# How a cached-attention and SwiGLU decode kernel loads w_down, the fourth group of wo, and its last tiles

## The chip, the cores and the metric

The kernel runs on one core of one Trainium2 chip. A core has TensorE (PE, matrix products into PSUM), VectorE (DVE), ScalarE (ACT), GpSimd (POOL) and SyncE (SP), which here does nothing but issue DMAs, and sixteen DMA engines that move data from HBM into SBUF. The metric is the device time of one execution in microseconds; the median of three runs counts.

## What is computed

One token is decoded. A is multi-head attention over a long cache, B a SwiGLU feed-forward block, and the output is a gated mix of both:

```python
g = sigmoid((x * gate_w).sum(-1))
q = (x @ wq).reshape(H, Dh)                   # 32 heads of 128, D = 512
scores = einsum("hd,hkd->hk", q, k_cache) * Dh**-0.5
o = einsum("hk,hkd->hd", softmax(scores), v_cache)   # 65536 positions a head
a = o.reshape(H * Dh) @ wo                    # wo: 4096 x 512
b = (silu(x @ w_gate) * (x @ w_up)) @ w_down  # w_down: 1792 x 512
out = g * a + (1 - g) * b
```

All inputs are bf16. The K and V caches are 512 MiB each, and each of their bytes is used once; all weights together are some 14 MB.

## The kernel before

**Tiles.** The caches are cut into tiles of 128 partitions x 16384 elements (4 MB, 32 KB a partition); a head has four K tiles and four V tiles, and there are 128 of each. All tiles live in one ring of five buffers (`big`), which also holds wq, w_gate with w_up (`gu_t`), w_down (`wd_t`) and, at the end, the second half of wo (`wo_t`). A tile can be loaded when the tile five before it in the ring has been used up.

**Work on a tile.** For a K tile, VectorE multiplies by the query and halves the products three times (`products`, lines 240 and 244), and TensorE sums the rest with 16 matmuls against an identity (`scores`, line 254). After the fourth K tile of a head come maximum, exponentials and row sums (`row_max`, `exponentials`, `total`, `weight`). For a V tile, TensorE accumulates 32 matmuls (`values`, line 302) into `O_ps`, four positions and 512 columns at a time. After the fourth V tile of a head, `head_copy` (line 315, and 317 for the last head) brings `O_ps` to SBUF, `head_column` (lines 323 and 330) turns it into a scaled column `oT` by four small products, and `project` (line 335) multiplies it by this head's rows of wo and adds it to `a_ps`. The heads 0 to 15 are projected as they come, with wo in four groups of four heads (`wo_tiles`); the heads 16 to 31 are projected after the last V tile, with `wo_end`.

**Order.** The program is written in the order in which each engine is to work (`manual_schedule`); nothing is reordered. The list `steps` says which K tile and which V tile belong to a step; V runs one head behind K, and by step 40 and later some more. A step issues its K tile, then wo's group if it is due, then its V tile, all on SP's queue, and then the work. Step 2 issues w_down behind K tile 2, and places `feed_forward_mid` (line 209: the products with w_down); step 3 issues wo's first group; the fourth group is issued at V tile 40, between a K and a V tile.

**Completion signals.** The DMAs of the kernel take eight completion semaphores in turn (numbers 100, 102, 104 and 106 to 110 in the trace). A DMA that takes a semaphore waits, on SP, until the DMA that had it before, eight issues earlier, has landed in full. A DMA over 128 partitions raises its semaphore sixteen times in the trace, one over 8 partitions eight times.

**Where before and after differ.** `wd_sb` (lines 136 to 146) lies on 64 partitions, 28 rows of w_down on each, and is loaded by eight DMAs of 8 partitions (every fourth partition). The activations `hT` come on 128 partitions, 14 columns; two matmuls against every second column of the identity turn them into 64 partitions and 28 columns (`h_ps`, line 202), and 28 matmuls on 64 partitions follow. The last V tile is loaded in five pieces, the one before it in two; `wo_end` is loaded in five.

Of the kernel before, what the change touches and what calls it, by code (L numbers as in the profile page):

```python
# [8 lines left out]
ACT = mybir.ActivationFunctionType  # L9
ALU = mybir.AluOpType  # L10
AXIS = mybir.AxisListType
P = 128
# [3 lines left out]
NB = 128  # L16
# [9 lines left out]
def kernel(  # L26
# [14 lines left out]
    nc = tc.nc  # L41
    bf16 = mybir.dt.bfloat16
    f32 = mybir.dt.float32

    _, H, Sk, Dh = A_k_cache.shape
    D = A_x.shape[2]
    F = B_w_gate.shape[1]
    KT = D // P
    FT = F // P
    G = Sk // (NB * P)  # L50
    NBH = Sk // P
    N = H * G
# [4 lines left out]
    consts = ctx.enter_context(tc.tile_pool(name="consts", bufs=1))  # L57
# [7 lines left out]
    psum_m = ctx.enter_context(tc.tile_pool(name="psum_m", bufs=2, space=bass.MemoryType.PSUM))  # L65
# [3 lines left out]
    def big(name):  # L69
        return ring.tile([P, NB * Dh], bf16, name=name, tag="big")  # L70
# [12 lines left out]
    ident_b = consts.tile([P, P], bf16, name="ident_b")  # L83
# [14 lines left out]
    a_ps = psum_a.tile([1, D], f32, name="a_ps")  # L98

    K_tiles, V_tiles, S_tiles, P_tiles, O_tiles = {}, {}, {}, {}, {}  # L100

    def load(dst, cache, n, name, cuts=(0, NB)):
        h, g = divmod(n, G)
        t = big(name)
        view = t.rearrange("p (j d) -> p j d", d=Dh)
        src = cache[0, h, g * NB * P : (g + 1) * NB * P, :].rearrange("(p j) d -> p j d", j=NB)
        for a, b in zip(cuts[:-1], cuts[1:]):
            nc.sync.dma_start(out=view[:, a:b, :], in_=src[:, a:b, :])
        dst[n] = view
# [24 lines left out]
    nc.sync.dma_start(out=wgu_sb[:, 0], in_=B_w_gate.rearrange("(p t) f -> p t f", t=KT))  # L134
    nc.sync.dma_start(out=wgu_sb[:, 1], in_=B_w_up.rearrange("(p t) f -> p t f", t=KT))
    wd_t = big("wd_t")
    HP = P // 2
    GT = F // HP
    wd_sb = wd_t[:HP, : GT * D].rearrange("p (t n) -> p t n", t=GT)
    wd_rows = B_w_down.rearrange("(p t) n -> p t n", t=GT)  # L140

    def load_wd(*which):
        for i in which:
            lo = (0, 1, 2, 3, 32, 33, 34, 35)[i]
            part = slice(lo, lo + 29, 4)
            nc.sync.dma_start(out=wd_sb[part], in_=wd_rows[part])

    with nc.allow_non_contiguous_dma(reason="small"):
        nc.sync.dma_start(out=gwT, in_=gate_w.rearrange("(p t) -> p t", t=KT))
    load_wd(0, 1)  # L150
    WG = 4
    wo_tiles = {}

    WH = H // 2
    wo_end = []

    def load_wo_end(cuts):
        t = big("wo_t")[:, : (H - WH) * D].rearrange("p (h n) -> p h n", n=D)
        rows = A_wo[WH * P :, :].rearrange("(h p) n -> p h n", p=P)
        for a, b in zip(cuts[:-1], cuts[1:]):  # L160
            nc.sync.dma_start(out=t[:, a:b, :], in_=rows[:, a:b, :])
        wo_end.append(t)

    def load_wo(g):
        wo_tiles[g] = wo_pool.tile([P, WG, D], bf16, name="wo_sb")
        rows = A_wo[g * WG * P : (g + 1) * WG * P, :]
        nc.sync.dma_start(out=wo_tiles[g], in_=rows.rearrange("(h p) n -> p h n", p=P))

    def feed_forward_in():

# [18 lines left out]
    def feed_forward_mid(gu_sb, eg):  # L189
        nc.vector.tensor_scalar_add(eg, eg, 1.0)  # L190
        nc.vector.reciprocal(eg, eg)
        hprod = consts.tile([P, FT], f32, name="hprod")
        nc.vector.tensor_tensor(out=hprod, in0=gu_sb[:, :FT], in1=eg, op=ALU.mult)
        hT = consts.tile([P, FT], bf16, name="hT")
        nc.vector.tensor_tensor(out=hT, in0=hprod, in1=gu_sb[:, FT:], op=ALU.mult)
        xg = consts.tile([P, KT], f32, name="xg")
        nc.vector.tensor_tensor(out=xg, in0=xT, in1=gwT, op=ALU.mult)
        xs = consts.tile([P, 1], f32, name="xs")
        nc.vector.tensor_reduce(out=xs, in_=xg, axis=AXIS.X, op=ALU.add)
        h_ps = psum_m.tile([HP, GT], f32, name="h_ps", tag="misc")  # L200
        for r in range(2):
            nc.tensor.matmul(
                h_ps[:, r * FT : (r + 1) * FT], lhsT=ident_b[:, r::2], rhs=hT, start=True, stop=True
            )
        h2 = consts.tile([HP, GT], bf16, name="h2")
        nc.scalar.activation(out=h2, in_=h_ps, func=ACT.Copy)
        b_ps = psum_m.tile([1, D], f32, name="b_ps", tag="misc")
        for t in range(GT):
            nc.tensor.matmul(  # L209
                b_ps, lhsT=h2[:, t : t + 1], rhs=wd_sb[:, t, :], start=(t == 0), stop=(t == GT - 1)  # L210
            )
        g_ps = psum_m.tile([P, 1], f32, name="g_ps", tag="misc")
        nc.tensor.matmul(g_ps, lhsT=ones_f, rhs=xs, start=True, stop=True)
        eg2 = consts.tile([P, 1], f32, name="eg2")
        nc.scalar.activation(out=eg2, in_=g_ps, func=ACT.Exp, scale=-1.0)
        return b_ps, eg2
# [13 lines left out]
    def products(n, a=0, b=NB):  # L230

        h = n // G
        K = K_tiles[n][:, a:b, :]
        qb = q_bc[:, h * Dh : (h + 1) * Dh]
        q_rep = bass.AP(
            tensor=qb.tensor,
            offset=qb.offset,
            ap=[list(qb.ap[0]), [0, b - a], [1, Dh]],
        )
        yield nc.vector.tensor_tensor(out=K, in0=K, in1=q_rep, op=ALU.mult)  # L240
        half = Dh
        while half > WIDTH:
            half //= 2
            yield nc.vector.tensor_tensor(  # L244
                out=K[:, :, 0:half], in0=K[:, :, 0:half], in1=K[:, :, half : 2 * half],
                op=ALU.add,
            )
# [43 lines left out]
    def weight(h, tot_ps):  # L291
        recip = small.tile([P, 1], f32, name="recip")
        nc.vector.reciprocal(recip, tot_ps)  # L293
        nc.vector.tensor_tensor(out=rg[:, h : h + 1], in0=recip, in1=gval, op=ALU.mult)
# [39 lines left out]
    def project(h):  # L334
        nc.tensor.matmul(  # L335
            a_ps,
            lhsT=oT[:, h : h + 1],
            rhs=wo_tiles[h // WG][:, h % WG, :] if h < WH else wo_end[0][:, h - WH, :],
            start=False,
            stop=(h == H - 1),  # L340
        )
# [3 lines left out]
    v = 0  # L345
# [9 lines left out]
    for n, v in steps:  # L355
        if n is not None and n > 1:
            load(K_tiles, A_k_cache, n, "K_t")
        if n == 2:
            load_wd(2, 3, 4, 5, 6, 7)
        if n == 3:  # L360
            load_wo(0)
        if v is not None:
            if v % (WG * G) == 2 * G and v // (WG * G) + 1 < WH // WG:
                load_wo(v // (WG * G) + 1)
            load(V_tiles, A_v_cache, v, "V_t", (0, NB) if v < N - 2 else (0, 64, NB) if v < N - 1 else (0, 32, 64, 96, 112, NB))
            if v == N - 1:
                load_wo_end((0, 4, 8, 12, 14, 16))
        if n == 2:
            ff = feed_forward_mid(*ff)
        halves = (0, NB // 2)  # L370
        vector = iter(()) if n is None else products(n)
        if n == 0:
            vector = (i for a in halves for i in products(n, a, a + NB // 2))
        top_of = None
        if n is None:
            top_of = H - 1 if S_tiles else None
        elif n % G == 0 and n > 0:
            top_of = n // G - 1
            vector = (i for a in halves for i in products(n, a, a + NB // 2))
        if top_of is not None:  # L380
            next(vector, None)
            mT_ps = row_max(top_of)
            next(vector, None)
            exponentials(top_of, mT_ps)
        for _ in vector:
            pass
        if n == 1:
            ff = feed_forward_in()
        if n == 3:
            feed_forward_out(*ff)  # L390
        if tot_ps is not None:
            weight(*tot_ps)
            tot_ps = None
        if done is not None:
            head_column(done, head_copy(done))
        if v is not None:
            values(v)
        if top_of is not None:
            tot_ps = top_of, total(top_of)
        if n is not None:  # L400
            scores(n)
        if done is not None and done < WH:
            project(done)
        done = v // G if v is not None and v % G == G - 1 else None
    O_last = head_copy(H - 1, last=True)
    for h in range(WH, WH + 4):
        project(h)
    head_column(H - 1, O_last)
    for h in range(WH + 4, H):
        project(h)  # L410

    out_sb = consts.tile([1, D], bf16, name="out_sb")
    nc.vector.tensor_copy(out=out_sb, in_=a_ps)
    nc.sync.dma_start(out=out[0], in_=out_sb)


# [28 lines left out]
```

## Time and profile before

| what | value |
|---|---|
| median of 3 runs | 2534.58 us (2534.54 to 2534.76) |
| the profiled execution | 2534.51 us, of it 2532.6 us from the first to the last instruction |
| VectorE busy | 2175.5 us (86% of the span) |
| TensorE busy | 1742.4 us (69%), mean granted clock 0.749 |
| ScalarE busy | 75.9 us (3%) |
| DMA | 1088.63 MB in 42884 packets, mean 430 GB/s |

A profile page gives, for each engine, the busy time, and then the span in forty slices with a digit for the busy tenths of each. Its chain of work goes back from the last instruction, at each step to what released it. The other answers used are the chain in order of time (start, length, what), the timeline (start, length, engine, line, operation, and in brackets the idle time before it and what ended it), and windows, which give for each stretch the busy time and number of instructions of PE, PEld (weight loads), DVE, ACT and POOL, then TensorE's granted clock, the DMA engines' busy share and GB/s. "SPq" is SP's queue. L302 is line 302 of the kernel. The trace also records each DMA packet with its size, start and duration, and each rise of a completion semaphore.

The DMA issues of the kernel, with the size of one:

| tile | DMAs | KB each |
|---|---|---|
| K_t | 127, and 2 halves | 4096, 2048 |
| V_t | 126, 2 halves, 3 and 2 smaller | 4096, 2048, 1024, 512 |
| wo_sb | 4 | 512 |
| wd_t | 8 | 224 |
| wo_t | 3 and 2 | 512, 256 |

### The profile page before, as it was taken

Reading aid. Unit: us, or ns where it says so; the run is one execution under the profiler, and the core shown is the slowest. Engines: PE = TensorE matmul, PEld = TensorE weight load, DVE = VectorE, ACT = ScalarE, POOL = GpSimd, SP = SyncE. Lnnn points to the kernel's source line nnn. Section 1 sums busy time; section 2 is a strip of 40 time slices with the busy share of each in tenths; the row PEclk is TensorE's granted clock in tenths of the full one; section 3 lists DMA queues with packets and bytes.
Section 4 is the critical chain, followed back from the end, with each engine's and each line's share of the span. In section 5 each row is a group of like instructions: output and inputs, shape, how many; then the busy total and the mean of one; then the engine's idle time right before and its main releaser. Section 6 shows DMA issues by size and latency. Waiting matters only on the chain.

```text
span 2532.6 us, 15260 instructions
## 1 busy us (share of the span) xinstructions
PE 1742.4 (69%) x6738; PEld 712.1 (28%) x6738; DVE 2175.5 (86%) x784; ACT 75.9 (3%) x207; POOL 0.7 (0%) x6
## 2 busy tenths in 40 slices
PE   4677666776677666676776677667666776677679
PEld 2222222222222222222222223222222232222223
DVE  7998888888888999998888888888888888888860
ACT  1000000000000000000000000000000000000000
POOL 0000000000000000000000000000000000000000
PEclk7677777777777676677777777777777777777779
DMA  9999999999999999999999999999999999999998
GB/s 415 433 433 430 433 433 433 432 430 435 432 432 434 431 433 432 432 433 433 432 434 433 432 434 433 432 432 434 432 431 434 433 430 434 434 431 433 434 432 339
DMA packets 42884, 1088.63 MB, mean 430 GB/s; under 512 B 4737, under 2 KB 8834, under 8 KB 9090
## 3 DMA queue, kind: packets, MB, share of 16 engines
q1 hardware_dynamic: 42674, 1087.66, 99.7%
q8 instruction: 53, 0.87, 0.1%
q14 instruction: 13, 0.11, 0.0%
q10 hardware_dynamic: 144, 0.00, 0.0%
HBM read 1087.64 MB, written 0.00 MB: 429 GB/s over the span
## 4 chain that ended last, share of the span: by engine, by line
DMA 68%; PE 22%; DVE 10%; issue 1%; ACT 0%; DVEq 0%; SPq 0%
DMA V_t<-in_A_v_cache_dram 61%; PE O_ps L302 20%; DMA K_t<-in_A_k_cache_dram 5%; DVE K_t L240 5%; DVE K_t L244 5%; PE S_ps L254 1%; DMA wo_t<-in_A_wo_dram 1%; DMA wq_t<-in_A_wq_dram 0%; PE qg_ps L117 0%; DVE m L266 0%; PE oh_ps L323 0%; PE a_ps L335 0%; PE a_ps L227 0%; ACT P_sb L279 0%; DVE top L275 0%
## 5 line engine op out<-in xcount | busy, mean ns | idle before, releaser
L302 PE MATMUL O_ps<-V_t,P_sb 128*4 128x512 bf16 x4096 | 1157.3, 453 | 496.8 <-DMA V_t<-in_A_v_cache_dram 494.3
L240 DVE TENSOR_TENSOR K_t<-K_t,q_bc 128x16384 bf16<-128x16384 bf16 (+1 forms) x160 | 1117.2, 6983 | 254.4 <-DMA K_t<-in_A_k_cache_dram 232.9
L244 DVE TENSOR_TENSOR K_t<-K_t 128x4096 bf16<-128x4096 bf16 (+3 forms) x480 | 1030.9, 2148 | 14.3
L302 PEld LDWEIGHTS <-P_sb 128*4 128x4 bf16 x4096 | 393.9, 97 | 1241.0 <-issue 897.5
L254 PE MATMUL S_ps<-K_t,ident_b 128*128 128x128 bf16 x2048 | 466.0, 394 | 107.0 <-DVE K_t L244 106.9
L254 PEld LDWEIGHTS <-ident_b 128*128 128x128 bf16 x2048 | 227.6, 115 | 330.0 <-issue 140.2
L323 PE MATMUL oh_ps<-ident_f,O_sb 4*128 4x1 f32 x256 | 57.9, 343 | 74.1 <-ACT O_sb L315 74.1
L323 PEld LDWEIGHTS oh_ps<-ident_f,O_sb 4*128 4x128 f32 x256 | 55.2, 314 | 83.7 <-ACT O_sb L315 78.9
L270 PE MATMUL mT_ps<-diag,ones_f 128*128 128x128 f32 x64 | 23.6, 468 | 79.8 <-ACT diag L268 79.8
L268 ACT ACTIVATE diag<-ident_f,m 128x128 f32<-128x128 f32 x32 | 12.8, 401 | 2099.3 <-DVE m L266 2099.3
L317 DVE COPY O_sb<-O_ps 4x256 f32<-4x256 f32 x1 | 0.4, 414 | 52.1 <-ACT O_sb L315 52.1
L270 PEld LDWEIGHTS mT_ps<-diag,ones_f 128*128 128x128 f32 x64 | 14.7, 285 | 95.6 <-ACT diag L268 95.6
L266 DVE TENSOR_REDUCE m<-S_ps 128x1 f32<-128x512 f32 x32 | 21.9, 683 | 7.4 <-PE S_ps L254 7.4
L315 ACT ACTIVATE O_sb<-O_ps 4x512 f32<-4x512 f32 (+1 forms) x32 | 18.1, 566 | 131.0 <-PE O_ps L302 131.0
L279 ACT ACTIVATE P_sb<-S_ps,bias 128x512 bf16<-128x512 f32 x32 | 22.0, 687 | 1.0
L117 PE MATMUL qg_ps<-wq_t,X_bc 128*128 128x512 bf16 x32 | 8.6, 436 | 13.2 <-DMA wq_t<-in_A_wq_dram 13.2
L293 DVE RECIPROCAL recip<-tot_ps 128x1 f32<-128x1 f32 x32 | 5.1, 160 | 12.2 <-PE tot_ps L288 12.2
L209 PE MATMUL b_ps<-wd_t,h 64*1 64x512 bf16 x28 | 12.1, 629 | 4.3 <-DMA K_t<-in_A_k_cache_dram 4.3
L288 PEld LDWEIGHTS tot_ps<-rowsum,ones_f 128*128 128x128 f32 x64 | 9.5, 188 | 14.0 <-issue 14.0
L288 PE MATMUL tot_ps<-rowsum,ones_f 128*128 128x1 f32 x64 | 12.2, 260 | 0.0
L330 ACT ACTIVATE oT<-oh_ps,rg 128x1 bf16<-128x1 f32 x32 | 8.4, 263 | 76.6 <-PE oh_ps L323 76.6
L227 PE MATMUL a_ps<-b_sb,ones_f 1*1 1x512 f32 x2 | 1.9, 1032 | 12.1 <-ACT b_sb L226 12.1
(42 smaller groups left out, 73.8 us busy)
## 6 DMA issues: line engine op xcount, KB each, us to landing
K_t<-in_A_k_cache_dram SPq DMA_DIRECT2D x127, 4096.0 KB, 35.3
V_t<-in_A_v_cache_dram SPq DMA_DIRECT2D x126, 4096.0 KB, 29.1
wq_t<-in_A_wq_dram SPq DMA_DIRECT2D x1, 4096.0 KB
K_t<-in_A_k_cache_dram SPq DMA_DIRECT2D x2, 2048.0 KB, 16.8
V_t<-in_A_v_cache_dram SPq DMA_DIRECT2D x2, 2048.0 KB
V_t<-in_A_v_cache_dram SPq DMA_DIRECT2D x3, 1024.0 KB, 29.4
wo_sb<-in_A_wo_dram SPq DMA_DIRECT2D x4, 512.0 KB, 17.3
gu_t<-in_B_w_gate_dram SPq DMA_DIRECT2D x1, 1792.0 KB
```

The source lines that it names most:

```text
L209: nc.tensor.matmul(b_ps, lhsT=h2[:, t : t + 1], rhs=wd_sb[:, t, :], start=(t == 0), stop=(t == GT - 1))
L240: yield nc.vector.tensor_tensor(out=K, in0=K, in1=q_rep, op=ALU.mult)
L244: yield nc.vector.tensor_tensor(out=K[:, :, 0:half], in0=K[:, :, 0:half], in1=K[:, :, half : 2 * half], op=ALU.add,)
L254: nc.tensor.matmul(S_tiles[h][:, g * NB : (g + 1) * NB], lhsT=ident_b, rhs=K_tiles[n][:, :, c], start=(c == 0), stop=(c == WIDTH - 1),)
L266: nc.vector.tensor_reduce(out=m, in_=S_tiles[h], axis=AXIS.X, op=ALU.max)
L268: nc.scalar.activation(out=diag, in_=ident_f, func=ACT.Copy, scale=m)
L270: nc.tensor.matmul(mT_ps, lhsT=ones_f, rhs=diag, start=True, stop=True)
L279: nc.scalar.activation(out=P_tiles[h], in_=S_tiles[h], func=ACT.Exp, bias=bias, scale=scale, accum_out=rowsum[:, h : h + 1],)
L288: nc.tensor.matmul(tot_ps, lhsT=ones_f, rhs=rowsum[:, h : h + 1], start=True, stop=True)
L302: nc.tensor.matmul(O_tiles[h], lhsT=P_tiles[h][:, g * NB + j : g * NB + j + 4], rhs=V_tiles[n][:, j : j + 4, :], start=(g == 0 and j == 0) ...
L315: nc.scalar.activation(out=O_sb[:, :cut], in_=O_ps[:, :cut], func=ACT.Copy)
L323: nc.tensor.matmul(oh_ps, lhsT=O_sb[:, c * Dh : (c + 1) * Dh], rhs=ident_f[0:4, c : c + 1], start=(c == 0), stop=(c == 3),)
```

## The change

w_down moves to 128 partitions with 14 rows each and is loaded by one DMA behind K tile 2, the third K tile; the turn of `hT` goes, and 14 matmuls on 128 partitions take the place of 28 on 64. wo's fourth group (`g == 3`) is loaded by six DMAs of 112, 8, 4, 2, 1 and 1 partitions. The last V tile comes in three pieces (64, 48 and 16 of its 128 columns of 128 elements) and wo's second half in three (7, 6 and 3 heads). After the last V tile, the last head's column is made first, and then all sixteen products with wo; the output is copied half by VectorE, half by ScalarE.

```diff
     wd_t = big("wd_t")
-    HP = P // 2
-    GT = F // HP
-    wd_sb = wd_t[:HP, : GT * D].rearrange("p (t n) -> p t n", t=GT)
-    wd_rows = B_w_down.rearrange("(p t) n -> p t n", t=GT)
-
-    def load_wd(*which):
-        for i in which:
-            lo = (0, 1, 2, 3, 32, 33, 34, 35)[i]
-            part = slice(lo, lo + 29, 4)
-            nc.sync.dma_start(out=wd_sb[part], in_=wd_rows[part])
+    wd_sb = wd_t[:, : FT * D].rearrange("p (t n) -> p t n", t=FT)
...
-    load_wd(0, 1)
...
     def load_wo(g):
         wo_tiles[g] = wo_pool.tile([P, WG, D], bf16, name="wo_sb")
         rows = A_wo[g * WG * P : (g + 1) * WG * P, :]
-        nc.sync.dma_start(out=wo_tiles[g], in_=rows.rearrange("(h p) n -> p h n", p=P))
+        rows = rows.rearrange("(h p) n -> p h n", p=P)
+        cuts = (0, P) if g < WH // WG - 1 else (0, 112, 120, 124, 126, 127, 128)
+        for a, b in zip(cuts[:-1], cuts[1:]):
+            nc.sync.dma_start(out=wo_tiles[g][a:b], in_=rows[a:b])
...
-        h_ps = psum_m.tile([HP, GT], f32, name="h_ps", tag="misc")
-        for r in range(2):
+        b_ps = psum_m.tile([1, D], f32, name="b_ps", tag="misc")
+        for ft in range(FT):
             nc.tensor.matmul(
-                h_ps[:, r * FT : (r + 1) * FT], lhsT=ident_b[:, r::2], rhs=hT, start=True, stop=True
-            )
-        h2 = consts.tile([HP, GT], bf16, name="h2")
-        nc.scalar.activation(out=h2, in_=h_ps, func=ACT.Copy)
-        b_ps = psum_m.tile([1, D], f32, name="b_ps", tag="misc")
-        for t in range(GT):
-            nc.tensor.matmul(
-                b_ps, lhsT=h2[:, t : t + 1], rhs=wd_sb[:, t, :], start=(t == 0), stop=(t == GT - 1)
+                b_ps,
+                lhsT=hT[:, ft : ft + 1],
+                rhs=wd_sb[:, ft, :],
+                start=(ft == 0),
+                stop=(ft == FT - 1),
             )
...
         if n == 2:
-            load_wd(2, 3, 4, 5, 6, 7)
+            nc.sync.dma_start(out=wd_sb, in_=B_w_down.rearrange("(p t) n -> p t n", t=FT))
...
-            load(V_tiles, A_v_cache, v, "V_t", (0, NB) if v < N - 2 else (0, 64, NB) if v < N - 1 else (0, 32, 64, 96, 112, NB))
+            load(V_tiles, A_v_cache, v, "V_t", (0, NB) if v < N - 2 else (0, 64, NB) if v < N - 1 else (0, 64, 112, NB))
             if v == N - 1:
-                load_wo_end((0, 4, 8, 12, 14, 16))
+                load_wo_end((0, 7, 13, 16))
...
     O_last = head_copy(H - 1, last=True)
-    for h in range(WH, WH + 4):
+    head_column(H - 1, O_last)
+    for h in range(WH, H):
         project(h)
-    head_column(H - 1, O_last)
-    for h in range(WH + 4, H):
-        project(h)
 
     out_sb = consts.tile([1, D], bf16, name="out_sb")
-    nc.vector.tensor_copy(out=out_sb, in_=a_ps)
+    nc.vector.tensor_copy(out=out_sb[:, : D // 2], in_=a_ps[:, : D // 2])
+    nc.scalar.activation(out=out_sb[:, D // 2 :], in_=a_ps[:, D // 2 :], func=ACT.Copy)
     nc.sync.dma_start(out=out[0], in_=out_sb)
```

## The prediction

> **What bounds the kernel now.** First the page's busy shares in forty slices, to ask whether the transfers or an engine are full.
>
> ```profile
> DMA  9999999999999999999999999999999999999998
> GB/s 415 433 433 430 433 433 433 432 430 435 432 432 434 431 433 432 432 433 433 432 434 433 432 434 433 432 432 434 432 431 434 433 430 434 434 431 433 434 432 339
> ```
>
> The sixteen DMA engines are full to the last slice. So what counts is the bytes that each must move, and the last one to finish. Next the chain of waits over the last 57 us (start, length, what), which sets the end.
>
> ```profile
> 2472.70 31.39 DMA V_t<-in_A_v_cache_dram
> ...
> 2504.16 20.87 DMA wo_t<-in_A_wo_dram
> 2525.03 0.04 issue
> 2525.07 1.02 PE a_ps L335 x4
> 2526.09 0.98 PE oh_ps L323 x8
> 2527.07 2.69 PE a_ps L335 x12
> 2529.76 0.02 issue
> 2529.79 0.68 DVE out_sb L413
> ```
>
> The gate is V tile 125, issued at 2472.70 and landed at 2504.09; call that landing L. The chain then names wo, but the timeline (start, length, engine) shows TensorE just as late:
>
> ```profile
> 2504.14 20.88 PE L302 MATMUL O_ps<-V_t,P_sb 128*4 128x512 bf16 x96 [1.62 <-DMA V_t<-in_A_v_cache_dram]
> 2525.11 0.37 ACT L315 ACTIVATE O_sb<-O_ps 4x256 f32<-4x256 f32 x1 [29.29 <-PE O_ps L302]
> 2525.52 0.41 DVE L317 COPY O_sb<-O_ps 4x256 f32<-4x256 f32 x1 [52.13 <-ACT O_sb L315]
> ```
>
> From L, TensorE runs tiles 125 to 127 without a break (96 starts 0.216 us apart). So the end is L + 28.5 us, and two questions remain: where L goes, and what the tail behind it becomes.
>
> Why is L late? Each 128-partition load raises sixteen completion signals, one for each DMA engine. The trace's records give those of tile 125:
>
> ```
> 2487.52 2487.56 | 2494.24 2494.27 2494.35 2494.36 2494.56 2494.78 2495.28 2495.92 2495.97 2496.01 2496.59 | 2500.18 2503.01 2504.09
> ```
>
> The mean is 2495.5; the load waits for one engine that is 8.5 us behind it. Two sources of the spread can be followed in the records. **w_down:** its loads raise eight signals, not sixteen, 1.06 us apart (53.89, 54.95, 56.02, ...), and its packets (28,672 bytes, 1.062 us, 64 of them) are all on eight engines. K tile 3, queued behind them, lands at 60.10 to 60.53 on eight engines and at 68.44 to 69.96 on the other eight. Call the late eight A, the others B. **Instruction loads:** 53 packets of 16,384 bytes (0.88 to 0.97 us), one every 48 us, go round eight engines. Following the packets from engine to engine (each starts where the last ended, within 4 ns), two of these eight are in A and six in B; each visit delays its engine by 0.95 to 1.4 us. At tile 125 A's latest is 2504.09 (w_down and instruction loads), B's latest 2496.01. No engine stood idle before 2508, not even the two that lead by 16.6 us, so loads are issued early enough for all.
>
> [...]
>
> **The change, part by part.**
>
> *w_down in one load.* A loses eight packets with their signals, 8 x 1.063 = 8.50 us; all sixteen gain eight packets of 14,336 bytes. The w_gate and w_up loads have just such rows: up lands 4.26 us behind gate (41.11 - 36.85). So A's latest goes from 2504.09 to 2504.09 - 8.50 + 4.26 = 2499.85, and B's latest from 2496.01 to 2500.27. B becomes the last. SP is freed too: before, it stood at w_down's issues until 43.20, where K tile 3 went out; now that issue waits for K tile 0's scores (PE, 35.58 + 3.65 = 39.2). This gains nothing, since the engines are busy with tile 2 and w_down until about 55. The h_ps turn (2 matmuls, 1 ACT copy) and 14 of 28 matmuls b_ps go, 6 us of TensorE near 60 to 72; the tile's slot comes free sooner, also worth nothing while no engine idles. If that cover were gone, it would be a gain.
>
> *wo's fourth group in six loads.* 512 packets of 1 KB stay the same 512. The 112-partition load gives each engine 7 partitions of 4 packets; the 8-partition one goes to A, as w_down's did, and I take the smaller ones to go there too. So a B engine carries 28 packets instead of 32. Packet pitch is 0.042 us (a 512-packet load per engine 1.36 us, from the landings 2525.03 and 2526.39): B's latest 2500.27 - 0.17 = 2500.10. A's engines take what B gives up: between 0 and 16 packets each, 0 to 0.7 us. For A's latest I take 0, and up to 0.25 us more would change nothing, since B is the last then (2500.10 against 2499.85); 0.7 stays in the range. **So the new L is 2500.10, 3.99 us earlier.** Six issues cost SP about 0.43 us each instead of one (row 841.24), and SP was waiting there anyway. But they use six of the eight signals. The V load behind them must now await the V load two before it, which lands at 860.97, and not be issued at 844.43. Behind it on SP stands only the next K load, issued at 862.20, which must now await the K load landing at 870.66. The slowest engine then still has a K tile (9.7 us) and 1.4 us of wo in front of it; others lead it there by about 5 us once w_down is even (12.4 before). I cost it at 0; were the lead over 11 us, an engine that is ahead would idle, which also costs nothing until it is the last.
>
> [...] The trace's eight small w_down loads follow each other at the 1.06 us of their packets, so queued loads here show no fixed cost. [...]
>
> *V tile 127 in three pieces, wo's second half in three.* On the slowest engine half a tile lies between L + 9.73 and L + 14.65, the piece to 112 at L + 18.33 (signals of the old cuts: 2513.82, 2518.74, 2522.42). TensorE is ready for tile 127 at L + 0.05 + 64 x 0.216 = L + 13.86, but must now wait for 64 columns, L + 14.70; 16 matmuls to 18.15; wait to 18.35; 16 matmuls, the last starting 15 x 0.216 later and taking 0.38: L + 21.97, where it was L + 20.93. That is **+1.04**. wo's last byte stays at about L + 25.0 (2529.11), and the 128 packets per engine need only that. Its issues come sooner: eight loads now fit the eight signals (before, SP's first wo issue waited for L itself).
>
> *All sixteen `project` behind `head_column`.* Before, four ran in the shadow of the O_sb copies (2525.07 to 2526.09). Now they follow: 4 x 0.216 = **+0.86**. wo's first seven heads (56 packets, 2.4 us behind L + 19.6) are there at L + 22.0, needed at L + 24.
>
> *out_sb halved.* ACT's half waits for DVE's in the instruction order, so 0.41 + 0.04 + 0.37 = 0.82 (the O_sb halves) for 0.68: **+0.14**. Bounds: 0.41 if side by side (-0.27), 0.82.
>
> Sum: -3.99 + 1.04 + 0.86 + 0.14 = -1.95. The profiled execution took 2534.51 (span 2532.6), 0.07 under the median 2534.58. 2534.51 - 1.95 = **2532.6**.
>
> **Rivals.**
> 1. *TensorE, not the load, sets the tail.* Before tile 125 it has only 1.62 us to spare. The granted clock alternates between 0.5 and 1.0 until 2467:
>
> ```profile
> 2420.00:2467.00 47.00, 30.36 (x116) 12.52 (x115) 31.30 (x10) 2.12 (x6) 0.00 (x0) 0.75 1.00 433
> 2467.00:2533.00 66.00, 60.40 (x284) 24.43 (x282) 1.42 (x4) 1.49 (x4) 0.00 (x0) 0.99 0.83 341
> ```
>
> (The clock is the third column from the right.) Matmuls start 0.427 us apart at the half clock. If its last stretch, 6.8 us, falls 4 us later against the work, 1.9 us more are lost; 1.6 are spare. With the load's gain only half passed on: 2534.6.
> 2. *Slower: the half clock returns in the tail.* Full clock held 65 us from 2467. The new tail ends later behind L (27.5 against 25.7 us); if the alternation of 10.2 us goes on there, two such stretches in 27.5 us each lose 5.1 us: 2532.6 + 10.2 = 2542.8; one alone gives 2537.7, within the bound. It decides from the second stretch on. Against it: VectorE, busy through the alternation, is done at 2453.
> 3. *The six small loads starve the queue.* Price up to one tile, 9.7 us: 2542. It decides only if the slowest engine idles, and it still holds a tile when the waits end.
> 4. *No shift of L*, if instruction loads land otherwise and leave the latest engine where it is: the tail alone, +2.0, 2536.6.
> 5. *Faster than reckoned*: instruction loads land more on the engines that lead, and L falls to the mean, 2495.5 (the bytes stay the same): -8.6 + 2.0 gives 2527.9.
>
> **How the numbers follow.** Forecast with its own bounds (L -4.2 to -3.5, tail +0.9 to +2.5; 2531.2 to 2533.5): 70. Rival 1: 12. One half-clock stretch: 5. Rival 4: 5. Rival 2: 3. Rival 3: 2. Rival 5: 3. The range must keep 80: forecast and rival 1, stretched to 2530.8 and 2535.6. This kernel's measurement can tell 0.2%, 5.1 us, from no change: faster (below 2529.5) 0.03, slower (above 2539.6) 0.05, between 0.92. The parts nearly cancel: a gain of 4 in the load, a loss of 2 in the tail.
>
> **What would show it.** K tile 3's sixteen signals within 2 us of each other, the last near 65.7. Tile 125's last signal near 2500.1, the sixteen spread over some 10 us and not 16.6, with six or more of them between 2498 and 2500.2. Then TensorE's breaks of 0.8 and 0.2 us in tile 127, no a_ps before oh_ps, 16 a_ps in one run of 3.6 us, and ACT after DVE on out_sb. I am wrong if L does not move, or if TensorE's clock in the tail is not full.

## The result, and the profile after

The changed kernel took **2545.22 us** (median of 5, 2544.74 to 2545.35) against 2534.58 us, a ratio of 1.0043 with a 95% interval of 1.0032 to 1.0054: 10.6 us slower. The forecast was 2532.6 us, in a range of 2530.8 to 2535.6. The profiled execution took 2544.87 us, of it 2543.1 us span.

The same two rows of the page, now of the kernel after, in forty slices of 63.6 us:

```profile
DMA  9999999999999999999999999999999999999998
GB/s 415 429 429 430 433 430 430 433 429 430 431 433 430 411 430 432 432 430 431 432 430 432 430 433 430 432 431 431 432 433 429 430 434 430 431 433 429 431 434 348
```

The busy shares are full, as before. The second row moved in two ways. Many slices stand two or three below those of before, through the whole span. And one slice, the fourteenth (827 to 890 us), has 411 where before had 431: that is where wo's fourth group is loaded. From 860 to 875 us the DMA engines' busy share is 1.00 at 327 GB/s, where before had 1.01 at 426: packets take longer there, and no engine is seen to wait.

The chain of waits of the kernel after, its last 44 us (start, length, what):

```profile
2497.28 34.14 DMA V_t<-in_A_v_cache_dram
2531.42 0.04 issue
2531.46 3.63 PE O_ps L292 x16
2535.09 0.02 issue
2535.11 0.02 ACTq L305
2535.13 0.04 issue
2535.17 0.38 ACT O_sb L305
2535.55 0.04 issue
2535.60 1.05 PE oh_ps L313 x8
2536.65 3.56 PE a_ps L325 x16
2540.20 0.02 issue
2540.23 0.42 DVE out_sb L401
2540.65 0.02 issue
2540.67 0.37 ACT out_sb L402
```

The tail has the shape that was forecast: the last 16 matmuls of tile 127 wait for its third piece, `oh_ps` comes ahead of every `a_ps`, sixteen `a_ps` run in 3.56 us, and ScalarE's half of the output follows VectorE's. It all comes 13 us too late, because L does. Tile 125's signals, from the records:

```
after: 2502.42 2502.52 2502.59 2502.63 2502.66 2503.99 2504.86 2509.09 2511.11 2511.25 2511.28 2511.30 2511.39 2512.67 2512.88 2513.03
```

Their spread is 10.6 us instead of 16.6 ("some 10 us" was forecast), and K tile 3's signals lie between 64.67 and 66.50, where before had two groups 8 us apart. So the engines were evened out as worked out. But L is 2513.03 and not 2500.10: **all sixteen are late together**, by about 13 us. The records of the 32 KB packets, 32,512 of them in each kernel, say where that comes from:

| kernel | at 1213 ns or less | 1214 to 1216 | 1217 to 1226 | longer | mean | sum / 16 engines |
|---|---|---|---|---|---|---|
| before | 32,363 | 21 | 23 | 105 | 1214.4 ns | 2467.6 us |
| after | 2,043 | 20,529 | 9,691 | 249 | 1219.3 ns | 2477.6 us |

Five nanoseconds on each of 2032 packets an engine are 10 us. Part of it is everywhere in the span, and part (packets of up to 2.3 us, and wo's 1 KB packets with a mean of 76.8 ns instead of 46.0) lies around 864 to 874 us.

### The profile page after: what moved, and what is told of

Same layout as the page of the kernel before. It is cut to its first block, busy times and chain, and to the rows that moved or that the text cites. A ratio compares the mean times of both kernels' runs of the same rounds, so it can differ in the third digit from the quotient of the medians.

```text
span 2543.1 us, 15216 instructions
## 1 busy us (share of the span) xinstructions
PE 1734.3 (68%) x6722; PEld 707.7 (28%) x6722; DVE 2175.2 (86%) x784; ACT 76.1 (3%) x207; POOL 0.7 (0%) x6
## 4 chain that ended last, share of the span: by engine, by line
DMA 67%; PE 22%; DVE 9%; issue 1%; ACT 0%; SPq 0%; DVEq 0%; ACTq 0%
DMA V_t<-in_A_v_cache_dram 62%; PE O_ps L292 21%; DMA K_t<-in_A_k_cache_dram 5%; DVE K_t L230 5%; DVE K_t L234 4%; PE S_ps L244 1%; PE oh_ps L313 0%; DVE m L256 0%; PE a_ps L325 0%; ACT P_sb L269 0%; PE a_ps L217 0%; ACT O_sb L305 0%; DVE top L265 0%; PE tot_ps L278 0%; PE mT_ps L260 0%
## 5 line engine op out<-in xcount | busy, mean ns | idle before, releaser
L265 DVE TENSOR_REDUCE top<-mT_ps 128x1 f32<-128x128 f32 x32 | 9.0, 282 | 1.3 <-PE mT_ps L260 1.3
```

## The experiments

**Theory.** Two things that the prediction did not price. First, the address: `h2`, a constant of 56 bytes a partition, is gone with the turn of `hT`; in the program of before it starts at byte 29,824 and the next constant at 29,888, 64 bytes on. The ring of big tiles, which lies behind the constants in SBUF, so moved from byte 30,976 (121 x 256) to byte 30,912 (192 above a multiple of 256), and each of its five buffers with it. Every packet of K and V writes there. Second, wo's fourth group, in six loads that cut the partitions, slows the packets around it. **Rivals:** the slower packets belong to an execution or a chip and not to the kernel; or w_down's new form, the instruction loads or the new tail make them.

All kernels below were timed in five rounds; times are medians, and ratios stand against runs of the kernel before on the same chip (2534.51 to 2534.73 us there). The kernel before varies more than most: its single executions there lie between 2533.06 and 2536.82 us.

### The address put back, the loads of wo whole, and both

In after_pad, 64 unused bytes a partition among the constants bring the ring back to byte 30,976:

```diff
     xT = consts.tile([P, KT], bf16, name="xT")
+    consts.tile([P, 32], bf16, name="pad")
```

In after_whole, the fourth group comes in one load again:

```diff
-        cuts = (0, P) if g < WH // WG - 1 else (0, 112, 120, 124, 126, 127, 128)
+        cuts = (0, P)
```

after_pad_whole has both edits.

> The changed kernel with 64 unused bytes per partition among the constants, so that the ring of big tiles starts at byte 30976 again (a multiple of 256, as before the change) and not at 30912. Theory 1, the start address of the tiles sets the pace: 32 KB packets go back from a mean of 1.217 us to 1.213 us, and with 2032 of them per engine and the instruction packets the time falls by 7 to 9 us, from 2545.2 to about 2537. Rival, the slower pace belongs to the chip or to the execution: no difference, 2545.

> The changed kernel with wo's fourth group in one load of 128 partitions. Theory 2, the load of 112 partitions and its small followers slow all packets near 864 to 874 us (1 KB packets 0.084 us instead of 0.046, 32 KB packets up to 2.3 us): 3 us less, 2542.2. Rival, those slow packets come from the instruction loads that fall there: no difference, 2545.

> The changed kernel with both edits: ring at byte 30976 and wo's fourth group in one load. Theories 1 and 2 together: 2533 to 2534.5, near the 2532.6 that was forecast for the change. If either theory is wrong, its part stays: 2537 (only the address counts) or 2542 (only the split counts).

| kernel | ring mod 256 | wo's fourth group | time | ratio to before | 32 KB mean | L |
|---|---|---|---|---|---|---|
| after | 192 | six loads | 2545.22 | 1.0043 [1.0032, 1.0054] | 1219.3 ns | 2513.03 |
| after_pad | 0 | six loads | 2534.51 | 1.0001 [0.9992, 1.0010] | 1215.2 ns | 2502.92 |
| after_whole | 192 | one load | 2542.00 | 1.0029 [1.0017, 1.0040] | 1218.1 ns | 2510.15 |
| after_pad_whole | 0 | one load | 2532.03 | 0.9990 [0.9982, 0.9999] | 1214.2 ns | 2500.45 |

Sixty-four unused bytes a partition take 10.7 us off with the six loads and 10.0 us with the one load, more than the 7 to 9 expected. One load instead of six takes off 3.2 us at the wrong address and 2.5 us at the right one. The two add up to the whole miss: with both undone the time is 2532.03 us where 2532.6 was forecast, and L is 2500.45 where 2500.10 was. The GB/s rows of after_pad and of after_pad_whole show the two causes apart:

```profile
GB/s 418 430 431 433 434 431 433 435 431 431 433 435 431 413 435 432 432 434 432 433 433 433 433 432 432 433 432 433 434 432 432 433 433 432 432 434 432 431 435 352
```

```profile
GB/s 418 431 431 432 434 434 431 432 432 434 433 432 432 432 434 432 432 432 435 432 432 433 434 433 431 433 434 433 432 432 434 433 432 431 435 434 430 432 435 352
```

With the address put back, the general level is that of before and the dip to 413 in the fourteenth slice stays; with one load the dip is gone too.

### The address alone, in the kernel before

The kernel before with unused bytes ahead of the ring; this is before_shift, with 192 of them, and before_128 and before_64 have 64 and 32 elements (128 and 64 bytes) in place of the 96:

```diff
     xT = consts.tile([P, KT], bf16, name="xT")
+    consts.tile([P, 96], bf16, name="pad")
```

> The kernel before with 192 unused bytes per partition among the constants: the ring starts at byte 31168, which is 192 above a multiple of 256, like the changed kernel's. Theory 1: packets of 1.217 us, and 7 to 9 us more than before, about 2542.5. Rival (chip or execution): 2534.6.

> The kernel before with 128 unused bytes a partition ahead of the ring, so that the ring of big tiles starts at a multiple of 128 and not of 256 bytes. If 256 is the step that counts, the 32 KB packets are slow as at 192 mod 256 (mean near 1218 ns, not 1214) and the time is near 2544.8. If any multiple of 128 will do, nothing changes: 2534.5. Half the harm, near 2540, would mean that the cost grows with the odd bytes.

> The kernel before with 64 unused bytes a partition ahead of the ring: its start is 64 mod 256. By a step of 256 or of 128 bytes it is slow, near 2544.8; by a step of 64 it would be 2534.5, but a start of 192 mod 256 was slow already, so this is not expected.

| kernel | ring mod 256 | time | ratio to before | 32 KB mean | L |
|---|---|---|---|---|---|
| before | 0 | 2534.5 to 2534.6 | | 1214.4 ns | 2504.09 |
| before_64 | 64 | 2543.44 | 1.0036 [1.0024, 1.0049] | 1218.2 ns | 2512.66 |
| before_128 | 128 | 2544.19 | 1.0037 [1.0024, 1.0049] | 1218.4 ns | 2512.40 |
| before_shift | 192 | 2544.85 | 1.0039 [1.0026, 1.0052] | 1218.3 ns | 2512.78 |

Nothing of the change is in these kernels, only unused bytes ahead of the ring, and 9 to 10 us are lost. So neither w_down's form, nor the instruction loads, nor the tail is needed for it, and the rival of a chance execution is out: each level comes back in every one of these kernels. The three starts off 256 cost the same within the spread of the runs (2542.86 to 2545.34 over the three), so how far off makes no difference here, and 64 or 128 is not the step that counts. All kernels without this loss start the ring at 30,976; no other multiple of 256 was run, so that 256 is the step is not shown. The small pools behind the ring moved by the same bytes as the ring in each kernel, and no run parts the two: that the ring counts rests on its packets, which grew. In before_shift's row there is no dip at the fourteenth slice; the loss is spread over all of them:

```profile
GB/s 416 430 431 429 430 432 433 429 429 431 432 431 431 429 431 434 430 430 434 431 429 434 431 429 432 432 430 431 432 431 430 431 432 431 430 432 430 431 430 341
```

The records of the profiled execution (2543.55 us, 9.0 more than that of before) agree in size: 1218.3 - 1214.4 = 3.9 ns by 2032 packets is 7.9 us on each engine, of the 8.7 us that L moved. Smaller packets grew as well (w_down's 28,672 bytes from 1062.0 to 1068.3 ns). Of before_shift's 32 KB packets 16,385 took 1215 ns and 6,463 took 1222. The loads read the same rows in both programs; it is the start in SBUF, where the data is written, that moved. Why a packet takes longer there is not shown.

### What in the six loads slows the packets

Four more ways to load the fourth group, each with the ring at 30,976 and the rest of the change. split_112_16, and split_64_64 with 64 in place of 112:

```diff
-        cuts = (0, P) if g < WH // WG - 1 else (0, 112, 120, 124, 126, 127, 128)
+        cuts = (0, P) if g < WH // WG - 1 else (0, 112, 128)
```

split_heads, with all 128 partitions and one head in each load:

```diff
-        cuts = (0, P) if g < WH // WG - 1 else (0, 112, 120, 124, 126, 127, 128)
+        cuts = (0, WG) if g < WH // WG - 1 else (0, 1, 2, 3, 4)
         for a, b in zip(cuts[:-1], cuts[1:]):
-            nc.sync.dma_start(out=wo_tiles[g][a:b], in_=rows[a:b])
+            nc.sync.dma_start(out=wo_tiles[g][:, a:b], in_=rows[:, a:b])
```

split_every4, with every fourth partition in each load:

```diff
-        cuts = (0, P) if g < WH // WG - 1 else (0, 112, 120, 124, 126, 127, 128)
-        for a, b in zip(cuts[:-1], cuts[1:]):
-            nc.sync.dma_start(out=wo_tiles[g][a:b], in_=rows[a:b])
+        n = 1 if g < WH // WG - 1 else 4
+        for i in range(n):
+            nc.sync.dma_start(out=wo_tiles[g][i::n], in_=rows[i::n])
```

> The changed kernel at the old ring address, wo's fourth group in two loads of 112 and 16 partitions, so that the four smallest loads are gone and the load with seven partitions for each engine stays. If what costs the 3 us is how 112 partitions fall on the sixteen engines (two engines writing near each other in SBUF), the time stays at the 2534.5 of six loads. If it is the small loads of 8, 4, 2, 1 and 1, it falls to the 2532.0 of one load.

> The changed kernel at the old ring address, wo's fourth group in two loads of 64 partitions. If several engines slow each other whenever a load reaches only some of the partitions at a time, both halves are slow, near 84 ns a packet instead of 46, and the time is 2533 to 2536. If only uneven shares or very small loads do harm, it is the 2532.0 of one load.

> The changed kernel at the old ring address, wo's fourth group in four loads of all 128 partitions, one head (1 KB a partition) each, so the 512 packets are the same and only the partitions are no longer cut. If cutting the partitions is what costs the 3 us, the packets stay at 46 ns and the time is the 2532.0 of one load. If it is the number of loads behind each other, it is 2534 to 2535 like the others with two and six.

> The changed kernel at the old ring address, wo's fourth group in four loads of 32 partitions, every fourth one in each (0, 4, 8, ...; then 1, 5, 9, ...). Before's w_down loads cut the partitions in just this way, 8 of them to a load and one to an engine, and kept their full rate (28,672 bytes in 1062 ns). If only cuts into ranges of neighbouring partitions do harm, the 1 KB packets stay near 47 ns and the time is the 2532.1 of four loads by heads. [...]

| the fourth group | loads | time | ratio to before | 1 KB packets, mean | stage |
|---|---|---|---|---|---|
| whole (after_pad_whole) | 1 | 2532.03 | 0.9990 [0.9982, 0.9999] | 47.0 ns | 30.39 us |
| by heads | 4 | 2532.11 | 0.9991 [0.9982, 1.0000] | 47.1 ns | 30.37 us |
| every fourth partition | 4 | 2532.08 | 0.9990 [0.9981, 0.9999] | 47.2 ns | 30.37 us |
| 64, 64 | 2 | 2535.50 | 1.0004 [0.9995, 1.0013] | 62.8 ns | 33.61 us |
| 112, 16 | 2 | 2534.91 | 1.0006 [0.9997, 1.0015] | 63.5 ns | 35.99 us |
| 112, 8, 4, 2, 1, 1 (after_pad) | 6 | 2534.51 | 1.0001 [0.9992, 1.0010] | 64.6 ns | 33.34 us |

"Stage" is the time from the landing of the second tile before the group to that of the second tile behind it, three tiles and the group; before has 30.39. The single executions of the first three kernels lie between 2531.91 and 2532.55 us, those of split_64_64 between 2534.92 and 2535.93, so the two levels are apart. The windows (length, busy time of PE, PEld, DVE, ACT and POOL, then TensorE's clock, the DMA engines' busy share and GB/s) of split_64_64 and, below it, of split_every4 show the same stretch:

```profile
860.00:875.00 15.00, 12.29 (x48) 5.15 (x49) 14.86 (x9) 1.57 (x4) 0.00 (x0) 0.84 1.01 349
```

```profile
860.00:875.00 15.00, 12.36 (x48) 5.12 (x49) 14.86 (x9) 1.57 (x4) 0.00 (x0) 0.84 1.03 432
```

The engines are full in both (1.01 and 1.03 on the row), but one moves 349 GB/s and the other 432. So it is not the number of loads (four cost nothing, two cost 3.4 us), not the small ones (64 and 64 is as dear as six with the smallest among them), and not the cutting of partitions as such: every fourth costs nothing. **Cuts into ranges of neighbouring partitions** do it in these kernels: 62.8 to 64.6 ns a packet, against 47.0 to 47.2 without them. In split_112_16 two of eleven executions were some 6 us longer still (2540.58 and 2541.26); the profile shows one of these, in which the 32 KB packets from 870 to 914 us took 1396 ns instead of 1213, so its stage is not the typical one. Fifteen per cent of these 44 us are about the 6 us lost.

Why neighbours? What split_64_64 was expected to take if several engines slow each other whenever a load reaches only some of the partitions came (2535.50 us, with packets of 62.8 ns rather than 84). But each load of split_every4 also reaches only some, 32 of 128, and its packets kept 47.2 ns, with the 2532.08 us expected if only neighbouring ranges do harm. So a load to some of the partitions is not enough for the loss, and the two rates above, 349 and 432 GB/s, go with which partitions each load takes. Which partition an engine carries is not in the records, and the mechanism is not shown.

### The two halves of the change that worked as reckoned

tail_alone is the kernel before with the four edits of the tail and nothing else; wdown_alone is after_pad_whole with the same four edits undone. For tail_alone:

```diff
-            load(V_tiles, A_v_cache, v, "V_t", (0, NB) if v < N - 2 else (0, 64, NB) if v < N - 1 else (0, 32, 64, 96, 112, NB))
+            load(V_tiles, A_v_cache, v, "V_t", (0, NB) if v < N - 2 else (0, 64, NB) if v < N - 1 else (0, 64, 112, NB))
...
-                load_wo_end((0, 4, 8, 12, 14, 16))
+                load_wo_end((0, 7, 13, 16))
...
-    for h in range(WH, WH + 4):
-        project(h)
     head_column(H - 1, O_last)
-    for h in range(WH + 4, H):
+    for h in range(WH, H):
         project(h)
...
-    nc.vector.tensor_copy(out=out_sb, in_=a_ps)
+    nc.vector.tensor_copy(out=out_sb[:, : D // 2], in_=a_ps[:, : D // 2])
+    nc.scalar.activation(out=out_sb[:, D // 2 :], in_=a_ps[:, D // 2 :], func=ACT.Copy)
```

> The changed kernel with the ring put back to the start address of before, wo's fourth group in one load, and the last tiles, the order of the projections and the output copy as before: so w_down in one load is all that is left of the change. If the balance of w_down is worth what the prediction said, tile 125's last signal comes near 2500.3 to 2500.5 as in the kernel with both undone, and the tail is 2.0 us shorter than there: 2530.0 to 2530.8. If the new tail costs nothing, as a rival has it, the time is the 2532.0 of the kernel with both undone.

> The kernel before with only the four edits of the tail: the last V tile in three pieces, wo's second half in three, all projections behind the last column, the output copied in two halves. The prediction's sum for the tail is +1.04 + 0.86 + 0.14 = +2.0: 2536.5, with tile 125's last signal unmoved near 2504. Rival: the tail is hidden elsewhere, 2534.5.

wdown_alone took **2530.60 us** (ratio 0.9986 [0.9977, 0.9994]), the fastest of all kernels here: 3.94 us less than the kernel before, for which L was to move by 3.99. Its L is 2500.26. tail_alone took 2535.99 us (ratio 1.0004 [0.9995, 1.0013]): +1.45 us where +2.0 was forecast, by itself not clear of the spread of before. After_pad_whole less wdown_alone is, and says the same: 2532.03 - 2530.60 = 1.43, from eleven executions each that, but for one, lie within 0.4 us.

wdown_alone's profiled execution took 2532.01 us, 1.4 us above the median, and its chain shows why:

```profile
2468.52 31.74 DMA V_t<-in_A_v_cache_dram
2500.26 0.04 issue
2500.30 22.57 PE O_ps L293 x96
```

Those 96 matmuls took 20.88 us in the profile before. The windows of the same execution (clock, third from the right):

```profile
2466.00:2472.00 6.00, 6.00 (x30) 2.41 (x29) 0.33 (x2) 0.00 (x0) 0.00 (x0) 1.00 1.01 434
...
2496.00:2500.00 4.00, 2.33 (x11) 0.85 (x10) 0.00 (x0) 0.00 (x0) 0.00 (x0) 1.00 0.95 401
2500.00:2504.00 4.00, 3.70 (x10) 1.19 (x10) 0.00 (x0) 0.00 (x0) 0.00 (x0) 0.57 0.99 422
2504.00:2522.00 18.00, 18.00 (x85) 7.07 (x84) 0.00 (x0) 0.00 (x0) 0.00 (x0) 1.00 0.86 339
```

In the first four microseconds behind L the granted clock was 0.57 on average, at a price of 1.7 us. This is not the last stretch of the alternation, which the first rival would have had fall later: the clock had been full from 2466 on, and the half clock came back for 3.4 us (the clock's records have it from 2500.4 to 2503.8). It is what the second rival named, in one short stretch. One of the eleven executions took that long; the other ten took 2530.45 to 2530.85 us, so the median is without it. Why it came in this one is not shown.

The tail's terms, from the timeline of tail_alone (start, length, engine, and in brackets the idle time before and its cause):

```profile
2526.08 0.37 ACT L315 ACTIVATE O_sb<-O_ps 4x256 f32<-4x256 f32 x1 [30.20 <-PE O_ps L302]
2526.48 0.41 DVE L317 COPY O_sb<-O_ps 4x256 f32<-4x256 f32 x1 [53.04 <-ACT O_sb L315]
2526.50 1.05 PE L323 MATMUL oh_ps<-ident_f,O_sb 4*128 4x1 f32 x8 [0.52 <-ACT O_sb L315]
2527.48 3.61 PE L335 MATMUL a_ps<-wo_t,oT 128*1 128x512 bf16 x16
```

`oh_ps` starts right behind ScalarE's half of the copy; it does not wait for VectorE's. Before, the four early `a_ps` held TensorE beyond that moment:

```profile
2525.07 1.02 PE L335 MATMUL a_ps<-wo_t,oT 128*1 128x512 bf16 x4
2526.02 1.05 PE L323 MATMUL oh_ps<-ident_f,O_sb 4*128 4x1 f32 x8
```

ScalarE's copy ended at 2525.48 there, and `oh_ps` came at 2526.02. So of the 1.02 us of the four products only about half lay in the shadow of the copy, and moving them behind costs only the other half.

## Why the prediction was wrong

*w_down in one load, -3.99.* Right: -3.94 in wdown_alone. The latest engines end close to each other, with eight of after_pad_whole's sixteen signals between 2498.50 and 2500.45, and L is within 0.4 us of the forecast in every kernel whose packets were not slowed (2500.13 to 2500.45).

*The step that failed first* is the one that was not written: the sum carried every packet's duration over from before. The prediction costed the turn of `hT` by its engine time and found its going "worth nothing while no engine idles"; that is so, but its 56 bytes of SBUF a partition held the ring at byte 30,976. Its move to 30,912 cost 10.0 to 10.7 us, five times the net gain forecast.

*wo's fourth group, "I cost it at 0".* It costs 2.5 us at the old address and 3.2 at the new. The working counted packets (512 before, 512 after) and took their pitch from a load of all partitions, 0.042 us; with the cut the 1 KB packets took 0.065 to 0.077 us, and 32 KB packets beside them up to 2.3 us. The third rival expected a loss here and named the wrong mechanism. The queue's issues do come as late as it said, as the timeline of SP in the kernel after shows:

```profile
841.67 10.10 SPq L160 DMA_DIRECT2D wo_sb<-in_A_wo_dram  x6
860.96 0.37 SPq L108 DMA_DIRECT2D V_t<-in_A_v_cache_dram  x1
873.20 0.35 SPq L108 DMA_DIRECT2D K_t<-in_A_k_cache_dram  x1
```

The next V load leaves at 860.96 (forecast 860.97) and the K load behind it at 873.20 instead of 862.20. That the first agrees to 0.01 us is luck: the forecast left out that w_down's gain moves this landing too, and in the kernel after the slower packets had eaten that gain by then. With the address put back the V load leaves at 857.01, 4 us earlier. But the DMA engines' busy share from 860 to 875 is 1.00: nothing shows an engine starved.

*The number of loads.* The prediction took from w_down's eight loads, 1.06 us apart, that queued loads show no fixed cost. None shows here either: split_heads has three loads more than after_pad_whole, of 128 KB each, and takes 0.08 us longer; after_pad has loads of 448, 32, 16, 8, 4 and 4 KB, split_112_16 of 448 and 64 KB, and after_pad takes no longer (2534.51 us against 2534.91).

*Tail, +2.04.* It was 1.43 to 1.45, and in the profiles of before and tail_alone: last `O_ps` behind L from 20.94 to 21.95, +1.01 (forecast 1.04); from there to the last `a_ps`, 4.73 to 5.11, +0.38 (forecast 0.86); output copies +0.13 (forecast 0.14). The mis-sized term is the projections, costed as if all four had run in the shadow of the copies.

*Rival 1* did not come: in after_pad_whole, where the load's gain is all there, TensorE was granted the full clock from 2466 on. *Rival 2*, the half clock in the tail, did not come in the kernel after either, whose clock was full from 2484 to 2541 although its work came 10 us later; one stretch of it came in the profiled execution of wdown_alone. *Rival 4*, no shift of L, is out by wdown_alone.

So the sum closes with the terms as measured, the address and then wo undone one after the other, and the tail by itself: 2532.6 + 10.7 (address) + 2.5 (wo) - 0.6 (tail) = 2545.2.

## What to carry to other kernels

In a kernel that its transfers bound, a removed or added constant can be an edit to every transfer: look where the buffers lie before and after, and time a move of their start by itself. Here a ring at byte 30,976 was 8.8 to 10.7 us faster, 0.4% of the whole time, than at 30,912, 31,040, 31,104 or 31,168. If a load amid others must be split, try columns (here by heads) or every fourth partition, which cost less than 0.1 us here (2532.11 and 2532.08 us against 2532.03), before ranges of neighbouring partitions, which cost 2.5 to 3.5 us, and even out the sixteen engines first where a few of them carried an uneven load (3.94 us here). And when a sum takes durations from a profile, ask of each what it depends on that the change moves.

## What the runs showed of the hardware that was not expected

- With the ring of the kernel before at byte 31,040, 31,104 or 31,168 (64, 128 and 192 above a multiple of 256) instead of 30,976, its 32 KB packets took 1218.2, 1218.4 and 1218.3 ns on average instead of 1214.4 (at 64 and 192 half of them took 1215 ns and a fifth 1222; at 128 they are spread differently, with a fifth at 1213 or less), and the time was 8.8 to 10.3 us longer; the three starts cost alike.
- With the fourth group's 1 KB rows loaded to ranges of neighbouring partitions (split_64_64, split_112_16, after_pad) their packets took 62.8, 63.5 and 64.6 ns instead of 47.0, and the core moved 349, 347 and 364 GB/s from 860 to 875 us instead of 436 (after_pad_whole); the same bytes to every fourth partition, or to all by columns, took 47.2 and 47.1 ns a packet, at 432 and 434 GB/s.
- Behind the load of 112 partitions in split_112_16 one profiled execution kept its 32 KB packets at 1396 ns for some 44 us, with the DMA engines' busy share at 1.00 from 875 to 895 us; a second of the eleven took as long. What starts or ends it was not tried.
- In one execution of wdown_alone's eleven TensorE's granted clock fell to a half for 3.4 us after 37 us of full clock, with VectorE idle since 2469.
